# Second batch's sums, sketches and numerators at other places among the down projections, and a weight chunk's splitting one unit sooner

## The chip, the cores and the metric

The kernel runs on one core of a Trainium2 chip. The metric is the device time of one execution in microseconds (us): the median of three runs of the kernel before is 279.8 us (279.78 to 281.41). Each engine of the core takes its own instructions from its own queue: PE (TensorE) multiplies matrices, DVE (VectorE) and ACT (ScalarE) do elementwise work and copies, POOL (GpSimd) does elementwise work between buffers in SBUF, and SP (SyncE) issues DMAs. PE writes its results to PSUM, which here is eight banks of 128 x 512 floats; the kernel calls two neighbouring banks a pair.

## The reference

```python
def phi(x):                        # sketched features, r*r = 64 per token
    a = np.einsum('rd,bhsd->bhsr', S1, x)
    b = np.einsum('rd,bhsd->bhsr', S2, x)
    return np.einsum('bhsi,bhsj->bhsij', a, b).reshape(*x.shape[:-1], r * r)
q_p, k_p = phi(q), phi(k)
kv  = np.einsum('bhsf,bhsd->bhfd', k_p, v)
z   = np.sum(k_p, axis=2)
num = np.einsum('bhsf,bhfd->bhsd', q_p, kv)
den = np.einsum('bhsf,bhf->bhs', q_p, z)[..., None] + 1e-06
x   = (num / den).transpose(0, 2, 1, 3).reshape(4352, 128)
g   = x @ w_gate                   # 128 x 1536
out = (g / (1 + np.exp(-g)) * (x @ w_val)) @ w_out
```

There are four batches of 4 heads x 1088 tokens x 32 channels. The output is 4352 x 128 in float32.

## The kernel before

The first batch's attention is done by itself at the start. From then on the feed-forward part (FFN) sets the pace, and the attention of the later batches is cut into steps that are placed between its pieces.

The tokens form blocks. Blocks 0, 1 and 2 are the first batch (384, 320 and 384 tokens); blocks 3 (`HEAD`) onward have 480 tokens each, the last one fewer. The 1536 hidden channels form 12 columns `j` of 128, and the weights are kept in four chunks of three columns. One unit is one block with one column: gate and value products, silu of the gate, and their product, which is a hidden slice. One `down` (line 1054) multiplies one hidden slice by its part of `w_out` and adds into the block's PSUM bank; the block's twelfth `down` is followed by `store` (line 1127), a DVE transpose and four DMAs on SP.

Units come in two forms. Those of blocks 0 and 1, and the first three of block 2, are plain float32 (`unit`, line 1017). From unit 3 of block 2 on, each product is the sum of faster fp32r products of split operands. `start_unit` (line 983) issues the two products with the difference parts and an ACT pass that negates the two banks (line 992). `finish_unit` (line 994) issues the four other products (lines 1001 and 1002), then ACT takes the silu (line 1004), and DVE makes the hidden slice (line 1009) and thereby frees the unit's pair. The split parts come from `cut_weights` (line 839), four steps for a chunk (ACT line 843, DVE or POOL line 846, ACT line 848, DVE or POOL line 855/851), and from `cut_tokens` (line 857) for a block: x1 on ACT (line 865), xd on DVE (line 873) and x0 on DVE or POOL (line 868). With `soon=True` the order is x1, xd, and in the next step x0.

No scheduler reorders anything: instructions stand in each engine's queue in the order in which the Python code issues them. A semaphore wait is added wherever an operand comes from another engine. A bank or buffer is reused only once its last reader is done; `pair` (line 122) hands out the pair that was least recently used among those not held.

The attention of batches 1 to 3 is the generator `attentions` (line 615), advanced one step by each `parts_of(1)` (line 1252). These steps of the second batch (batch 1) matter here:

- the step with the key sums: `key_values` (line 388), the third batch's `key_products` (line 354) and its ACT copies (line 590), `value_sums` (line 713, PE, which needs `zs`, the POOL sums of line 547), `fold` (DVE, lines 601 to 608, which makes the operand `s123` of the query sketches) and `spread_out` (a DVE transpose on line 723, six DMAs on SP, and four loads of the next values);
- the step with the query sketches: `query_sketches` (line 342, PE) and two ACT copies into `qab`;
- eight steps of `query_step` (line 737): scores and division (lines 741 to 748), then three times a product (line 377) and a transpose (line 758) on DVE, which fill `phT`;
- `numerators` (line 766): 64 small matmuls (line 776) into two pairs, then copies to `xT` (line 793) on ACT and DVE. These are the tokens of block 3 and beyond.

Three loops place all this. The first (`for z`, line 1327) runs the plain units. The second (`for n in range(ND)`, line 1354) has 19 `down`s; after the `down` numbered n it takes an attention step if n is in a listed set, and the splitting steps that `steps_at[n]` names ("x" is `cut_tokens` of block 2, "g3" and "v3" are chunk 3 of the gate and value weights). The third (`for j in range(3, NCH)`, line 1366) runs the nine split units of block 2. Its turn j starts unit j + 1, finishes unit j, takes a `down`, and then steps. A last `while` loop takes the rest of the `down`s and starts block 3.

Of the kernel before, what the change touches and what calls it, by code (L numbers as in the profile page):

```python
# [19 lines left out]
def kernel(  # L20
# [38 lines left out]
    NCH = Dff // P  # L59
# [62 lines left out]
    def pair(keep=None):  # L122

        i = min((i for i in (0, 4, 6) if i not in held), key=lambda i: max(used[i], used[i + 1]))
        touch(i, i + 1)
        if keep is not None:
            held.add(i)
            kept[keep] = i
        return PS[:, i : i + 2, :]
# [3 lines left out]
    def let_go(keep):  # L133
        i = kept.pop(keep)
        held.discard(i)
        touch(i, i + 1)
# [720 lines left out]
    def cut_tokens(i, engine=nc.gpsimd, soon=False):  # L857

        t0, n = blocks[i]
        x = xT[:, t0 : t0 + n]  # L860
        x1, x0, xd = x_parts[i] = [
            apool.tile([P, WB], F32R, tag=tag, name=name, bufs=2)
            for tag, name in (("qb", "x1"), ("dT", "x0"), ("rd", "xd"))
        ]
        nc.scalar.activation(x1[:, 0:n], x, AF.Copy, scale=CUT)  # L865

        def low():
            engine.tensor_tensor(  # L868
                out=x0[:, 0:n], in0=x, in1=whole(x1[:, 0:n]), op=ALU.subtract
            )  # L870

        def difference():
            nc.vector.scalar_tensor_tensor(
                out=xd[:, 0:n], in0=whole(x1[:, 0:n]), scalar=WHOLE, in1=x,
                op0=ALU.mult, op1=ALU.subtract,
            )


        first, second = (difference, low) if soon else (low, difference)
        first()  # L880
        yield
        second()
# [16 lines left out]
    def now(where, y):  # L899
        for f in where.pop(y, ()):  # L900
            f()
# [49 lines left out]
    def cut_hidden(y, i, j):  # L951

        if not h_sets:
            x = []
            for tag in ("kld", "qld", "vld", "kT", "qT"):
                t = const.tile([P, 2, WB], F32R, tag=tag, name="h" + tag, bufs=1)
                x += [t[:, k, :] for k in range(2)]
            t = const.tile([P, 8, WB], F32R, tag="late", name="hlate", bufs=1)
            x += [t[:, k, :] for k in range(8)]
            h_sets.extend(x[k : k + 3] for k in range(0, 18, 3))  # L960
        n = SPLIT if i == LAST else blocks[i][1]
        h_sets.append(h_sets.pop(0))
        h1, h0, hd = h_parts[i, j] = [x[:, 0:n] for x in h_sets[-1]]
        h = hidden[i, j][:, 0:n]
        if j in (2, 5, 8, 10) and i != line[2]:
            add_to(before, y + 1, lambda: nc.vector.tensor_scalar(h1, h, CUT, None, op0=ALU.mult))
        else:
            add_to(behind, y + 1, lambda: nc.scalar.activation(h1, h, AF.Copy, scale=CUT))  # L968
        add_to(before, y + 2, lambda: nc.gpsimd.tensor_tensor(  # L969
            out=h0, in0=h, in1=whole(h1), op=ALU.subtract  # L970
        ))
        add_to(before, y + 3, lambda: nc.vector.scalar_tensor_tensor(
            out=hd, in0=whole(h1), scalar=WHOLE, in1=h, op0=ALU.mult, op1=ALU.subtract
        ))
# [8 lines left out]
    def start_unit(i, j):  # L983

        n = blocks[i][1]
        xd = x_parts[i][2][:, 0:n]
        ps = sums_of[i, j] = pair((i, j))[:, :, 0:n]
        for k, w in enumerate((wg, wv)):
            nc.tensor.matmul(  # L989
                ps[:, k], w_parts[id(w), j // 3][2][:, j % 3, :], xd, start=True, stop=True  # L990
            )
        nc.scalar.activation(ps, ps, AF.Copy, scale=-1.0 / WHOLE)  # L992

    def finish_unit(i, j, y=None):
        n = blocks[i][1]
        x1, x0, _ = (x[:, 0:n] for x in x_parts[i])
        ps = sums_of.pop((i, j))
        now(before, y)
        for k, w in enumerate((wg, wv)):
            w1, wb = (w_parts[id(w), j // 3][t][:, j % 3, :] for t in range(2))  # L1000
            nc.tensor.matmul(ps[:, k], w1, x1, start=False, stop=False, skip_group_check=True)  # L1001
            nc.tensor.matmul(ps[:, k], wb, x0, start=False, stop=True, skip_group_check=True)  # L1002
        sg = fpool.tile([P, WB], FP32, tag="sg", name="sg", bufs=5)[:, 0:n]
        nc.scalar.activation(sg, ps[:, 0], AF.Silu, scale=WHOLE)  # L1004
        slot_of[i, j] = slots.pop(0)
        hj = slot_of[i, j]
        hidden[i, j] = hj
        todo.append((i, j))
        nc.vector.scalar_tensor_tensor(  # L1009
            out=hj[:, 0:n], in0=ps[:, 1], scalar=WHOLE, in1=sg, op0=ALU.mult, op1=ALU.mult  # L1010
        )
        let_go((i, j))
        now(behind, y)
        if (i, j) in DOWN:
            cut_hidden(y, i, j)
# [38 lines left out]
    def down(y=None):  # L1054

        i, j = todo.pop(0)
        n = SPLIT if i == LAST else blocks[i][1]
        first = i not in acc
        if first:
            acc[i] = bank("g2" if i == 1 or i in line[2::2] else "acc")  # L1060
        made[i] = made.get(i, 0) + 1
        mine = [c for c in range(NCH) if (i, c) in DOWN]
        if mine and j == mine[0]:
            acc[i, "p"] = bank("acc" if i in line[2::2] else "g2")
        sides = dict(start=first, stop=(made[i] == NCH))
        if j in mine:
            w1, wb, wd = [down_parts[x][:, FINE.index(j), :] for x in ("w1", "wb", "wd")]
            h1, h0, hd = h_parts.pop((i, j))
            nc.tensor.matmul(acc[i][:, 0:n], wd, hd, **sides)  # L1069
            p = acc[i, "p"][:, 0:n]  # L1070
            nc.tensor.matmul(p, w1, h1, start=(j == mine[0]), stop=False)  # L1071
            nc.tensor.matmul(p, wb, h0, start=False, stop=(j == mine[-1]))  # L1072
            if j == mine[-1]:
                copy_out(y, i, n)
        else:
            w = down_parts["scaled"][:, PLAIN.index(j), :] if mine else wo[:, j, :]
            nc.tensor.matmul(acc[i][:, 0:n], w, hidden[i, j][:, 0:n], **sides)  # L1077
        if i != LAST:
            hidden.pop((i, j))
            slots.append(slot_of[i, j])  # L1080
        if made[i] == NCH:
            if mine:
                put_together(y, i, n)
            elif i == HEAD - 1:

                add_to(behind, 1, lambda: store(i, n))
            else:
                store(i, n)
# [62 lines left out]
    def part(name, i):  # L1151

        next(fills[name, i], None)
# [47 lines left out]
    n = steps[0][1]  # L1201
# [50 lines left out]
    def parts_of(n):  # L1252

        for _ in range(n):
            if ahead[0] not in ("pe", "end"):
                ahead[0] = next(att, "end")
# [60 lines left out]
    def at(*names):  # L1317
        for name in names:
            next(cuts[name], None)

    def next_down():
        if order:
            todo.remove(order[0])
            todo.insert(0, order.pop(0))
        down()

    for z, (i, j) in enumerate(seq):
# [19 lines left out]

    steps_at = {
        0: ("v1", "v2"), 1: ("g1",), 2: ("g2",), 3: ("g1", "v1", "v2"), 4: ("g1",), 5: ("g1", "g2"), 6: ("g2", "v1"),
        7: ("g2", "v2"), 8: ("v3",), 9: ("g3",), 10: ("v0",), 11: ("g0",), 12: ("x",), 13: ("x",), 14: ("g3",),  # L1350
        15: ("g3",), 18: ("g3",),
    }
    ND = 19
    for n in range(ND):
        if n == ND - 2:
            start_unit(2, 3)
        next_down()
        for p in parts.pop(len(seq) + n, ()):
            part(*p)
        parts_of(n in (0, 1, 2, 3, 4, 11, 13, 15, 16, 17))  # L1360
        at(*steps_at.get(n, ()))


    steps_at = {4: ("v3",), 6: ("v3",), 7: ("v3",), 8: ("v0", "g0"), 9: ("v0", "g0"), 10: ("v0", "g0")}
    todo.sort(key=lambda x: (order + [x]).index(x))
    for j in range(3, NCH):
        if j + 1 < NCH:
            start_unit(2, j + 1)
        else:
            parts_of(1)  # L1370
            x_steps = cut_tokens(HEAD, nc.vector, soon=True)
            next(x_steps)
        finish_unit(2, j)
        next_down()
        parts_of(j < 8)
        if j == 4:


            lows["v3"][:] = [slots.pop().rearrange("p (c f) -> p c f", f=P)]
        at(*steps_at.get(j, ()))  # L1380
    while todo:
        if len(todo) == 2:
            start_unit(HEAD, 0)
        next_down()
        next(x_steps, None)
        parts_of(len(todo) > 0)

    flat = hbuf[:].rearrange("p s w -> p (s w)")
# [73 lines left out]
```

## Time and profile before

| quantity | value |
|---|---|
| median of the three runs | 279.8 us |
| the profiled execution's own time | 279.75 us |
| its span in the profile | 278.0 us |
| PE busy | 269.6 us (97% of the span) |
| DVE / ACT / POOL busy | 213.7 / 193.9 / 99.2 us |
| granted TensorE clock | full in all 40 slices |

The span runs from the first to the last recorded instruction, so 1.75 us of the execution lie around it. Times in a timeline count from the span's start. A row merges neighbouring instructions of one kind: start, length, engine, source line, operation, result and operands, shape, and count; brackets give the idle time of the engine just before the row and what ended it. For a float32 matmul PE shows two records per instruction, so "x4" on line 1077 is two `down`s. The records of successive matmuls overlap[...]: a row's start and the start of the next one tell more than its length.

### The profile page before, as it was taken

To read this page: it belongs to the slowest core of one execution; us is meant where nothing else is said; L and a number is where in the kernel's file an instruction comes from. 1 tells how busy PE (TensorE), PEld (TensorE's weight loads), DVE (VectorE), ACT (ScalarE), POOL (GpSimd) and SP (SyncE) were. 2 spreads that over 40 slices of the span, in tenths; PEclk is the share of its full clock that TensorE was granted. 3 is DMA by queue.
4 is the path that set the end of the run, shared out by engine and by line. 5 is a ranking of instruction groups with operands and counts; after the bars stand their busy time and mean duration, and the time that the engine had idled before them with its cause. 6 is when DMAs were issued, how large, how long until landed. Compare 5 with 4: busy or idle time off the path is not lost.

```text
span 278.0 us, 5775 instructions
## 1 busy us (share of the span) xinstructions
PE 269.6 (97%) x2193; PEld 201.4 (72%) x2193; DVE 213.7 (77%) x371; ACT 193.9 (70%) x348; POOL 99.2 (36%) x111
## 2 busy tenths in 40 slices
PE   8899999996999999999999999999999999999995
PEld 7645566664886677767667778767887888788994
DVE  3997988999896883787736667867986995978771
ACT  3468566444676676766568898859879888887880
POOL 3314322179020360080024352435335462633320
PEclk9999999999999999999999999999999999999999
DMA  6573195222250033200200010000100200010021
GB/s 194 165 229 95 37 283 170 83 80 83 60 90 0 4 61 90 58 0 0 35 13 6 4 30 6 0 2 8 28 2 0 35 1 0 12 26 1 5 33 28
DMA packets 26139, 14.30 MB, mean 51 GB/s; under 512 B 19840, under 2 KB 24192, under 8 KB 26112
## 3 DMA queue, kind: packets, MB, share of 16 engines
q1 hardware_dynamic: 25456, 13.84, 19.5%
q8 instruction: 17, 0.28, 0.4%
q10 hardware_dynamic: 656, 0.10, 0.2%
q14 instruction: 10, 0.08, 0.1%
HBM read 11.41 MB, written 2.23 MB: 49 GB/s over the span
## 4 chain that ended last, share of the span: by engine, by line
PE 86%; DVE 7%; POOL 2%; DMA 2%; issue 1%; ACT 1%; SPq 0%; DVEq 0%; ACTq 0%; POOLq 0%
PE PS L1077 17%; PE PS L1001 14%; PE PS L989 14%; PE PS L1002 13%; PE PS L1025 10%; PE PS L1069 3%; PE PS L1072 3%; PE PS L1071 3%; PE PS L776 2%; PE PS L342 2%; POOL zs L547 2%; DMA kld<-in_k_dram 2%; PE PS L354 1%; DVE phk L377 1%; PE PS L388 1%
## 5 line engine op out<-in xcount | busy, mean ns | idle before, releaser
L992 ACT ACTIVATE PS<-PS 128x960 f32<-128x960 f32 (+1 forms) x93 | 85.7, 922 | 33.0 <-PE PS L989 32.0
L1009 DVE SCALAR_TENSOR_TENSOR hbuf<-PS,sg 128x480 f32<-128x480 f32 (+1 forms) x93 | 58.5, 629 | 40.5 <-ACT sg L1004 38.3
L1004 ACT ACTIVATE sg<-PS 128x480 f32<-128x480 f32 (+1 forms) x93 | 51.1, 549 | 1.3 <-PE PS L1002 1.2
L1077 PE MATMUL PS<-hbuf,wo 128*128 128x480 f32 (+2 forms) x100 | 41.6, 518 | 0.0
L989 PE MATMUL PS<-xd,graw 128*128 128x480 f32 (+1 forms) x72 | 39.9, 554 | 0.0
L989 PE MATMUL PS<-xd,wd 128*128 128x480 f32 (+1 forms) x93 | 34.5, 371 | 0.2 <-DVE hbuf L1009 0.2
L1002 PE MATMUL PS<-x,wb 128*128 128x480 f32 (+1 forms) x93 | 34.5, 371 | 0.0
L1001 PE MATMUL PS<-x,w 128*128 128x480 f32 (+1 forms) x93 | 34.4, 370 | 0.0
L1002 PE MATMUL PS<-x,graw 128*128 128x480 f32 (+1 forms) x72 | 26.6, 369 | 0.0
L989 PEld LDWEIGHTS PS<-xd,wd 128*128 128x128 f32 x93 | 17.6, 189 | 11.3 <-issue 5.9
L1077 PEld LDWEIGHTS PS<-hbuf,wo 128*128 128x128 f32 x100 | 18.7, 189 | 5.1 <-issue 0.4
L1025 PE MATMUL PS<-xT,wg 128*128 128x384 f32 (+1 forms) x54 | 21.1, 472 | 0.1
L1025 PE MATMUL PS<-xT,wv 128*128 128x384 f32 (+1 forms) x54 | 20.7, 466 | 0.3 <-DVE wv L286 0.3
L1077 PE MATMUL PS<-hbuf,scaled 128*128 128x480 f32 (+1 forms) x48 | 20.7, 518 | 0.0
L868 POOL TENSOR_TENSOR x<-xT,x 128x480 fp32r<-128x480 f32 (+1 forms) x6 | 7.1, 1192 | 37.7 <-ACT x L865 37.7
L989 PEld LDWEIGHTS PS<-xd,graw 128*128 128x128 f32 x72 | 13.6, 189 | 8.1 <-ACT PS L992 4.1
L1001 PEld LDWEIGHTS PS<-x,w 128*128 128x128 f32 x93 | 17.5, 188 | 2.2
L1002 PEld LDWEIGHTS PS<-x,wb 128*128 128x128 f32 x93 | 17.5, 188 | 2.1
L969 POOL TENSOR_TENSOR hlate<-hbuf,hlate 128x480 fp32r<-128x480 f32 (+1 forms) x12 | 14.3, 1198 | 11.4 <-ACT hlate L968 9.3
L1001 PE MATMUL PS<-x,graw 128*128 128x480 f32 (+1 forms) x48 | 18.1, 376 | 0.0
L1029 ACT ACTIVATE sg<-PS 128x384 f32<-128x384 f32 (+1 forms) x21 | 9.6, 462 | 11.1 <-PE PS L1025 11.1
L1001 PE MATMUL PS<-x,gphq 128*128 128x480 f32 (+1 forms) x45 | 17.0, 377 | 0.0
(201 smaller groups left out, 546.7 us busy)
## 6 DMA issues: line engine op xcount, KB each, us to landing
kld<-in_k_dram SPq DMA_DIRECT2D x4, 544.0 KB, 4.2
vld<-in_v_dram SPq DMA_DIRECT2D x12, 144.0 KB, 5.2
qld<-in_q_dram SPq DMA_DIRECT2D x3, 544.0 KB, 4.0
raw<-in_moe_w_out_dram SPq DMA_DIRECT2D x4, 384.0 KB, 4.4
raw<-in_moe_w_gate_dram SPq DMA_DIRECT2D x3, 384.0 KB, 3.7
raw<-in_moe_w_val_dram SPq DMA_DIRECT2D x3, 384.0 KB, 3.5
out_dram<-o SPq DMA_DIRECT2D x16, 60.0 KB, 2.0
vld<-in_v_dram SPq DMA_DIRECT2D x4, 112.0 KB, 4.2
```

The lines of the kernel that those rows point to most:

```text
L969: add_to(before, y + 2, lambda: nc.gpsimd.tensor_tensor(out=h0, in0=h, in1=whole(h1), op=ALU.subtract))
L989: nc.tensor.matmul(ps[:, k], w_parts[id(w), j // 3][2][:, j % 3, :], xd, start=True, stop=True)
L992: nc.scalar.activation(ps, ps, AF.Copy, scale=-1.0 / WHOLE)
L1001: nc.tensor.matmul(ps[:, k], w1, x1, start=False, stop=False, skip_group_check=True)
L1002: nc.tensor.matmul(ps[:, k], wb, x0, start=False, stop=True, skip_group_check=True)
L1004: nc.scalar.activation(sg, ps[:, 0], AF.Silu, scale=WHOLE)
L1009: nc.vector.scalar_tensor_tensor(out=hj[:, 0:n], in0=ps[:, 1], scalar=WHOLE, in1=sg, op0=ALU.mult, op1=ALU.mult)
L1025: nc.tensor.matmul(o[:, 0:n], w[:, j, :], xT[:, t0 : t0 + n], start=True, stop=True)
L1029: nc.scalar.activation(sg[:, 0:n], g[:, 0:n], AF.Silu)
L1069: nc.tensor.matmul(acc[i][:, 0:n], wd, hd, **sides)
L1071: nc.tensor.matmul(p, w1, h1, start=(j == mine[0]), stop=False)
L1077: nc.tensor.matmul(acc[i][:, 0:n], w, hidden[i, j][:, 0:n], **sides)
```

## The change

The step with the key sums is taken after `down` 13 in place of 11 of the second loop. The query sketches follow after `down` 16 in place of 13, so three `down`s lie between the two steps in place of two. The remaining attention steps of that loop follow after 17 and 18. The first step of "x" (x1 and xd) is issued with n = 11 and the second (x0) with n = 12, in place of 12 and 13. In the third loop the attention steps go on through j = 8. The numerators come at j = 10, in front of the end of unit 10 and the start of unit 11, with two `down`s behind it, where before they came at j = 11, in front of the end of unit 11. The splitting steps of "v3" are taken at j = 3, 5 and 6 in place of 4, 6 and 7, and one "g0" step moves from j = 10 to j = 9. x0 of block 3 is issued at the end of turn j = 11, where before the `while` loop issued it. Nothing is added or removed: every product, copy and DMA is the same as before.

```diff
-        7: ("g2", "v2"), 8: ("v3",), 9: ("g3",), 10: ("v0",), 11: ("g0",), 12: ("x",), 13: ("x",), 14: ("g3",),
+        7: ("g2", "v2"), 8: ("v3",), 9: ("g3",), 10: ("v0",), 11: ("g0", "x"), 12: ("x",), 14: ("g3",),
         15: ("g3",), 18: ("g3",),
     }
...
-        parts_of(n in (0, 1, 2, 3, 4, 11, 13, 15, 16, 17))
+        parts_of(n in (0, 1, 2, 3, 4, 13, 16, 17, 18))
         at(*steps_at.get(n, ()))
...
-    steps_at = {4: ("v3",), 6: ("v3",), 7: ("v3",), 8: ("v0", "g0"), 9: ("v0", "g0"), 10: ("v0", "g0")}
+    steps_at = {3: ("v3",), 5: ("v3",), 6: ("v3",), 8: ("v0", "g0"), 9: ("v0", "g0", "g0"), 10: ("v0",)}
     todo.sort(key=lambda x: (order + [x]).index(x))
+    x_steps = iter(())
     for j in range(3, NCH):
-        if j + 1 < NCH:
-            start_unit(2, j + 1)
-        else:
+
+        alone = j == NCH - 2
+        if alone:
             parts_of(1)
             x_steps = cut_tokens(HEAD, nc.vector, soon=True)
             next(x_steps)
-        finish_unit(2, j)
-        next_down()
-        parts_of(j < 8)
-        if j == 4:
+            finish_unit(2, j)
+        if j + 1 < NCH:
+            start_unit(2, j + 1)
+        if not alone:
+            finish_unit(2, j)
+        for _ in range(1 + alone):
+            next_down()
+        parts_of(j < 9 or j == NCH - 1)
+        if j == 3:
             lows["v3"][:] = [slots.pop().rearrange("p (c f) -> p c f", f=P)]
         at(*steps_at.get(j, ()))
+        if j == NCH - 1:
+            next(x_steps, None)
     while todo:
         if len(todo) == 2:
             start_unit(HEAD, 0)
         next_down()
-        next(x_steps, None)
         parts_of(len(todo) > 0)
```

As built, the queues of the changed kernel differ from those of the kernel before at these places. On PE two `down`s of 384 tokens stand in front of the key products in place of behind the value sums, and three of 320 tokens stand between the value sums and the query sketches in place of behind the sketches. On DVE xd, x0 and the store transpose of block 0 stand in front of the fold. On ACT a gate weight's split and x1 stand in front of the two copies of the key sketches. On SP the four output DMAs of block 0 stand in front of the six `spread` DMAs and the four value loads.

## The prediction

> **What bounds the kernel now.** I read the page first, then PE's timeline around the moved steps, then DVE's and ACT's over the same stretch. The page says that the end is set by PE:
>
> ```profile
> PE 269.6 (97%) x2193; PEld 201.4 (72%) x2193; DVE 213.7 (77%) x371; ACT 193.9 (70%) x348; POOL 99.2 (36%) x111
> PE 86%; DVE 7%; POOL 2%; DMA 2%; issue 1%; ACT 1%; SPq 0%; DVEq 0%; ACTq 0%; POOLq 0%
> ```
>
> So a moved step gains or loses only what it does to PE's gaps. In the moved stretch PE shows these:
>
> ```profile
> 62.80 1.21 PE L388 MATMUL PS<-phk,vld 128*32 128x64 f32 x72
> 63.94 0.80 PE L354 MATMUL PS<-s,kT 128*64 128x64 f32 x20
> 65.15 0.69 PE L354 MATMUL PS<-s,kT 128*64 128x64 f32 x16 [0.41 <-DVE kT L327]
> 67.66 0.32 PE L713 MATMUL PS<-zs,ones 128*32 128x64 f32 x8 [1.82 <-POOL zs L547]
> 67.91 1.56 PE L1077 MATMUL PS<-late,wo 128*128 128x384 f32 x4
> 69.39 1.69 PE L342 MATMUL PS<-s,qT 128*32 128x96 f32 x72
> 71.02 1.88 PE L1077 MATMUL PS<-late,wo 128*128 128x320 f32 x6
> 72.49 0.58 PE L989 MATMUL PS<-xd,graw 128*128 128x384 f32 x1
> ...
> 87.65 2.35 PE L776 MATMUL PS<-phT,spread 32*32 32x288 f32 x64
> ...
> 97.61 0.48 PE L989 MATMUL PS<-xd,wd 128*128 128x480 f32 x1 [0.23 <-DVE hbuf L1009]
> ```
>
> The reader is to see two gaps before the first split unit, 0.41 + 1.82 = 2.23 us, and that PE goes from the value sums to the sketches without one: the two downs at 67.91 hide the fold. From 72.49 to 87.65 there is no gap. The numerators take 2.28 us (87.65 to 89.93) where the fourth batch's take 1.49 (185.34 to 186.83 in the chain): 0.79 of it is a stall, since their second pair is freed by the DVE product that runs from 87.88 to 88.44 below. DVE and ACT over the same time:
>
> ```profile
> 67.05 0.97 DVE L851 SCALAR_TENSOR_TENSOR graw<-room,graw 128x384 fp32r<-128x384 f32 x1
> 68.04 0.23 DVE L601 TENSOR_TENSOR fold<-PS,sq 128x64 f32<-128x64 f32 x1
> ...
> 68.88 0.24 DVE L723 STREAM_TRANSPOSE spread<-PS 128x64 f32<-128x64 f32 x1
> 70.27 0.56 DVE L873 SCALAR_TENSOR_TENSOR xd<-x,xT 128x384 fp32r<-128x384 f32 x1 [1.15 <-ACT x L865]
> 70.74 0.58 DVE L1131 STREAM_TRANSPOSE o<-PS 128x384 f32<-128x384 f32 x1
> 71.24 0.52 DVE L868 TENSOR_TENSOR x<-xT,x 128x384 fp32r<-128x384 f32 x1
> ...
> 87.88 0.56 DVE L1009 SCALAR_TENSOR_TENSOR hbuf<-PS,sg 128x384 f32<-128x384 f32 x1 [1.37 <-ACT sg L1004]
> ```
>
> ```profile
> 68.72 0.68 ACT L590 COPY kab<-PS 128x320 f32<-128x320 f32 x2
> 69.29 0.53 ACT L843 ACTIVATE gphq<-wg 128x384 fp32r<-128x384 f32 x1
> 69.72 0.52 ACT L865 ACTIVATE x<-xT 128x384 fp32r<-128x384 f32 x1
> ```
>
> The fold starts 0.02 us after DVE's previous work. xd waits for ACT's x1, which is late because ACT itself was waiting for DVE before 67.05.
>
> **What the Trainium skill says.** "Perfetto Trace Analysis", section on the Tensor Engine instruction: DVE, ACT and GpSimd take their queues strictly in order, and a matmul's end is a computed one. The first decides this case, and the trace agrees as far as it can: no DVE row overtakes xd in its 1.15 us wait. The second is why I count from start to start. "SBUF — State Buffer", "Who interferes with whom": DVE and GpSimd share a port pair under an exclusive lock. The trace agrees: the weight remainder (line 846) took 1.62 us beside GpSimd's sums at 62.85, and 0.55 at 71.68 without them.
>
> **The change, part by part.** Every instruction exists before; only waits change.
>
> *Two downs in front of the key sums.* A down of 384 tokens costs 0.65 us in the chain, so the key products start at 62.80 + 1.30 = 64.10. They take 1.14 and the key sketches 1.2, the end being 66.44; kT is ready at 65.10, so the 0.41 gap goes. The POOL queue is unchanged and zs still lands at 67.61, so PE waits 1.2 in place of 1.82 and the value sums start at 67.66 as before. The gain is the 1.30 us of downs that no longer follow.
>
> *Three downs behind the value sums.* 320 tokens cost 0.54 each, 1.62 together: PE reaches the sketches at 67.91 + 1.62 = 69.53.
>
> *x1, xd and x0 sooner.* The sketches need the fold, and the fold now stands on DVE behind xd, x0 and the store of block 0. ACT, released at 67.05, has one more weight split in front of x1: starts 0.42 apart (67.05, 67.48, 67.89, 68.31, 68.72) put x1 at 69.14 and its end at 69.66. DVE idles from 68.02 until then. xd at 69.69, x0 at 70.16, store at 70.62 and fold at 71.12 follow with the old starts' spacing (0.47, 0.44 to 0.50). The fold's chain lasted 0.92 (68.04 to 68.96), which ends at 72.04. PE therefore waits from 69.53 to about 72.05, 2.5 us. Behind it stand all split units; behind the fold on DVE the spread transpose and the scores. The sketches (1.63) end at 73.68 and the first split product follows, not at 72.49: 1.2 late. In terms: 1.30 of downs gained in front, 2.5 of wait paid. Bounds of the wait: x1 follows four splits on an ACT that is released at 67.05, at 0.41 or more each, so x1 can hardly end before 69.4 and the wait is at least 2.2; if the three DVE steps slow as beside GpSimd (0.97 against 0.55), it is at most 3.5.
>
> *SP.* The four stores are issued at about 0.5 us each (eight took 3.95 at 76.11), so the spread DMAs end near 78 plus 3.7 to land at worst. The numerators need them at 87; the value loads are needed at 100. Cost nothing; without that cover, up to 2 us.
>
> *Query step.* The ACT copies end 2.24 after the sketches' start (71.63 - 69.39), hence 74.3; the scores follow 2.1 later than before. The weight step and unit 3's product now stand ahead of the feature products, so unit 3's product is at 77.1, when its silu is ready (75.91 + 1.2). Products and transposes (0.87 each) alternate with the 1.69 us units and catch up: the last transpose runs 85.9 to 86.8 behind unit 8's product.
>
> *Chunk 3's GpSimd steps.* wd (line 855) ended at 82.35, just before its product at 82.37, with no gap. Sooner gains nothing, and at worst GpSimd's 1.0 us lands beside another DVE product (1.80 in place of 0.96 at 81.37), which the slack before 85.4 takes.
>
> *Numerators in front of unit 10.* PE gets there at 87.73 - 1.69 + 1.2 = 87.2. Their second pair is unit 9's, whose DVE product stands behind the transpose and two weight remainders (0.46 and 0.5): it starts near 87.75 and ends near 88.3. The stall is 1.1 in place of 0.79, +0.3. Afterwards all three pairs are taken, so unit 11's first product waits for ACT's copies (0.81 after the end of the numerators, PE arriving at 0.80: +0.06), and unit 11's finish waits for ACT's pass behind copies, x1 and a silu (ends 2.65 after; PE arrives at about 2.5: +0.2). Block 3's start has 4.7 us of cover in place of 2.45, but no gap was there. The gap of 0.23 at 97.61, where DVE was late with the key features, mostly vanishes as PE is later: -0.2.
>
> *Sum.* 1.2 + 0.3 + 0.26 - 0.2 = 1.56 us. From 98 us on PE is full and nothing takes it back. The profiled execution becomes 279.75 + 1.56 = 281.3; its 279.75 is within 0.05 of the 279.8 median, so the same number stands for both.
>
> **The rivals.** (1) The gain comes as drawn: the fold is not held. Then the first split product is 1.33 early (67.91 + 1.62 + 1.63 = 71.16), and with 0.3 + 0.26 later the time is 279.75 - 1.33 + 0.56 = 279.0; 278.4 if those are absent too. For it: PE's two gaps are real. Against: x1's end at 69.66. (2) Slower, over 1%: the late scores make phT late. If GpSimd's lock stretches two feature products by 0.9 each behind the wait, the last transpose ends near 88.3, unit 9's product near 89.8, and the numerators stall 2.5 (+1.7); with the 0.26 behind them and no recovery at 97.61 that is 1.2 + 1.7 + 0.26 = 3.1, or 282.9. It decides once unit 9's product ends 1.1 us later than the 88.3 above. For it: 1.80 us seen at 81.37. Against: each unit leaves DVE 0.4 us spare. (3) The second half gives it back: DVE has caught up, unit 9's product ends before PE arrives at 87.2, and the old stall goes: 1.2 - 0.79 - 0.2 = +0.2, 280.0. Against: the two weight remainders stand in front of that product, which puts its end at 88.3.
>
> **How the numbers follow.** Main case 0.62, rival 1 0.09, rival 2 0.2, rival 3 0.09. The main case with its wait of 2.2 to 3.5 gives 281.0 to 282.3. The range 279.4 to 282.8 adds rival 3 and the near part of rival 2, and leaves out rival 1 and some 0.1 of rival 2. A change under 1% can hardly be told from none: faster (below 277.0) 0.02, within 0.78, slower (above 282.6) 0.20.
>
> **What would show it.** In the profile after: a gap in front of line 342 of about 2.5 us whose releaser is DVE, xd on DVE ahead of the fold with a wait on ACT line 865 of about 1.6 us, the gap before line 713 down to 1.2, and the numerators at 2.5 us or more. I am wrong if line 342 starts before 71, or if the numerators take over 3.3 us.

## The result, and the profile after

The changed kernel takes 281.6 us (median of 20 runs, 280.94 to 282.96), the kernel before beside it 281.49 us (20 runs, 279.60 to 282.54). The ratio is 1.0021 with a 95% interval of 1.0001 to 1.0041: some 0.6 us slower, and within 1%. The profiled execution of the changed kernel took 280.94 us with a span of 279.2 us, where the one of before took 279.75 with 278.0: 1.2 us more.

One fact is needed to read these numbers: in part of the executions the granted TensorE clock dips for a short time, which shows as a mean clock of 0.988 to 0.994 in place of 0.998 or more, and these are about 1.5 us longer. Of the changed kernel, 11 of 20 executions ran at the full clock (median 281.22) and 9 had a dip (282.73). For these 20 of the kernel before only times are on record: 4 lie at 279.6 to 280.2 (median 279.79) and 16 at 281.3 to 282.5, which I take for executions with a dip. The times alone don't part them sharply: of 46 later executions of that kernel at the full clock, 10 took over 281 us as well. Like against like the change costs 1.2 us (the two profiles, both at the full clock) to 1.4 (the medians). It reads as 0.6 in the whole because fewer of its executions have a dip. Where the dips come from is tried below.

The page of the changed kernel still names PE, with the same work:

```profile
PE 269.7 (97%) x2193; PEld 200.8 (72%) x2193; DVE 213.2 (76%) x371; ACT 194.2 (70%) x348; POOL 99.4 (36%) x111
```

PE's timeline of the changed kernel, over the moved steps (start, length, line, operation, result and operands, idle time before and its releaser):

```profile
63.94 1.21 PE L388 MATMUL PS<-phk,vld 128*32 128x64 f32 x72
65.08 1.27 PE L354 MATMUL PS<-s,kT 128*64 128x64 f32 x36
67.49 0.32 PE L713 MATMUL PS<-zs,ones 128*32 128x64 f32 x8 [1.14 <-POOL zs L547]
67.73 1.88 PE L1077 MATMUL PS<-late,wo 128*128 128x320 f32 x6
71.77 1.69 PE L342 MATMUL PS<-s,qT 128*32 128x96 f32 x72 [2.15 <-DVE s L608]
73.39 0.44 PE L989 MATMUL PS<-xd,graw 128*128 128x384 f32 x1
...
86.72 0.68 PE L776 MATMUL PS<-phT,spread 32*32 32x288 f32 x6
87.89 1.51 PE L776 MATMUL PS<-phT,spread 32*32 32x256 f32 x58 [0.50 <-DVE hbuf L1009]
```

The two gaps of before, 0.41 and 1.82 us, have become one of 1.14. A new one of 2.15 stands in front of the query sketches, released by the last DVE instruction of the fold. DVE and ACT show why the fold is so late:

```profile
66.89 0.96 DVE L851 SCALAR_TENSOR_TENSOR graw<-room,graw 128x384 fp32r<-128x384 f32 x1
69.51 0.57 DVE L873 SCALAR_TENSOR_TENSOR xd<-x,xT 128x384 fp32r<-128x384 f32 x1 [1.66 <-ACT x L865]
70.00 0.55 DVE L868 TENSOR_TENSOR x<-xT,x 128x384 fp32r<-128x384 f32 x1
70.47 0.57 DVE L1131 STREAM_TRANSPOSE o<-PS 128x384 f32<-128x384 f32 x1
70.97 0.18 DVE L601 TENSOR_TENSOR fold<-PS,sq 128x64 f32<-128x64 f32 x1
71.19 0.27 DVE L605 TENSOR_REDUCE w<-fold 128x8 f32<-128x64 f32 x1
71.49 0.22 DVE L608 TENSOR_TENSOR s<-w,own 128x64 f32<-128x64 f32 x1
...
86.39 0.52 DVE L846 TENSOR_TENSOR room<-wv,w 128x384 f32<-128x384 f32 x1
86.83 0.55 DVE L846 TENSOR_TENSOR room<-wg,gphq 128x384 f32<-128x384 f32 x1
87.29 0.55 DVE L1009 SCALAR_TENSOR_TENSOR hbuf<-PS,sg 128x384 f32<-128x384 f32 x1
```

```profile
68.55 0.51 ACT L843 ACTIVATE gphq<-wg 128x384 fp32r<-128x384 f32 x1
68.97 0.51 ACT L865 ACTIVATE x<-xT 128x384 fp32r<-128x384 f32 x1
```

The value sums start at 67.49, so the fold could have started near 67.9 (before it started 0.38 us behind them). It stands behind xd, which waits 1.66 us for x1, behind x0 and behind the store. At 86.39 two weight remainders stand in front of unit 9's product, which ends at 87.84, and only then does the larger part of the numerators run.

The first stage differs by up to 1.6 us from one profiled execution to the next, so I count each from the first row of its last plain unit (line 1025, 128x320). The end of the count is the third batch's key products. Two rows of before, then two of the changed kernel:

```profile
53.78 0.81 PE L1025 MATMUL PS<-xT,wg 128*128 128x320 f32 x2
100.21 1.21 PE L388 MATMUL PS<-phk,vld 128*32 128x64 f32 x72
...
53.63 0.81 PE L1025 MATMUL PS<-xT,wg 128*128 128x320 f32 x2
101.38 1.21 PE L388 MATMUL PS<-phk,vld 128*32 128x64 f32 x72
```

The starts of PE's rows then are:

| us after the last plain unit | before | after | difference |
|---|---|---|---|
| key products with the values, line 388 | 9.02 | 10.31 | +1.29 |
| value sums, line 713 | 13.88 | 13.86 | 0.0 |
| query sketches, line 342 | 15.61 | 18.14 | +2.53 |
| first split product, line 989 | 18.71 | 19.76 | +1.05 |
| length of the numerators' stretch | 2.28 | 2.61 | +0.33 |
| end of the numerators to block 3's first product | 2.45 | 4.49 | +2.04, of it 1.69 a unit that now lies there |
| third batch's key products, line 388 | 46.43 | 47.75 | +1.32 |

### The profile page after: what moved, and what is told of

The parts are those of the page before. It is cut to its first block, busy times and chain, and to the rows that moved or that the text cites. A ratio compares the mean times of both kernels' runs of the same rounds, so it can differ in the third digit from the quotient of the medians.

```text
span 279.2 us, 5778 instructions
## 1 busy us (share of the span) xinstructions
PE 269.7 (97%) x2193; PEld 200.8 (72%) x2193; DVE 213.2 (76%) x371; ACT 194.2 (70%) x348; POOL 99.4 (36%) x111
## 4 chain that ended last, share of the span: by engine, by line
PE 86%; DVE 9%; ACT 1%; DMA 1%; issue 1%; SPq 0%; ACTq 0%; DVEq 0%
PE PS L1077 17%; PE PS L1001 14%; PE PS L989 14%; PE PS L1002 14%; PE PS L1025 10%; PE PS L1072 3%; PE PS L1071 3%; PE PS L1069 3%; PE PS L776 2%; PE PS L342 2%; DMA kld<-in_k_dram 1%; PE PS L354 1%; DVE room L846 1%; PE PS L388 1%; DVE man L277 1%; PE PS L1117 1%
```

## Experiments: the hold in front of the sketches

**The token split behind the fold.** This moves x1, xd and x0 so far that the sums' step is issued ahead of them.

```diff
-        ... 11: ("g0", "x"), 12: ("x",), 14: ("g3",),
+        ... 11: ("g0",), 13: ("x",), 14: ("x", "g3"),
```

> Block 2's token split one down later than the changed kernel has it, so that x1, xd and x0 stand behind the fold in their queues; all else as changed. My theory (the fold is held on DVE behind xd, which waits for x1): the 2.15 us gap in front of the query sketches goes, since only the store transpose (0.57) stands in front of the fold and the three downs (1.62) hide both. The first split unit starts 2.2 us sooner than in the changed kernel and 1.2 sooner than before; the numerators still stall, so the span is 279.2 - 2.1 = 277.1 and the time about 278.8. Rival (the gap comes from elsewhere, from the downs moved in front or from zs): the gap stays at 1 us or more and the span within 0.7 us of 279.2.

Measured: 279.87 us (20 runs), ratio to before 0.9952 (0.9935 to 0.9968), span 278.5. PE and DVE of this kernel:

```profile
68.15 0.32 PE L713 MATMUL PS<-zs,ones 128*32 128x64 f32 x8 [1.15 <-POOL zs L547]
68.40 1.88 PE L1077 MATMUL PS<-late,wo 128*128 128x320 f32 x6
70.47 1.69 PE L342 MATMUL PS<-s,qT 128*32 128x96 f32 x72 [0.18 <-DVE s L608]
...
74.40 0.44 PE L1001 MATMUL PS<-x,gphq 128*128 128x384 f32 x1 [0.27 <-ACT PS L992]
```

```profile
68.94 0.18 DVE L601 TENSOR_TENSOR fold<-PS,sq 128x64 f32<-128x64 f32 x1
69.16 0.27 DVE L605 TENSOR_REDUCE w<-fold 128x8 f32<-128x64 f32 x1
69.46 0.95 DVE L608 TENSOR_TENSOR s<-w,own 128x64 f32<-128x64 f32 x1
```

The gap of 2.15 is down to 0.18, and the first split product comes 17.81 us after the last plain unit in place of 19.76: 1.95 sooner, with 2.2 expected. The 0.18 is left because line 608 took 0.95 us here and 0.22 in the changed kernel: GpSimd is splitting weights (line 855) at that time. The third batch's key products come at 46.35, 1.40 sooner and not 2.1. The missing 0.5 is the wait at 74.40: unit 3's end follows its predecessor by 0.60 where it was 0.17, and its next product follows by 0.28 where it was 0.18. PE got there before ACT had done the sketches' copies and the negation:

```profile
72.30 0.52 ACT L848 ACTIVATE graw<-room 128x384 fp32r<-128x384 f32 x1 [1.56 <-DVE room L846]
72.73 0.92 ACT L590 COPY qab<-PS 128x480 f32<-128x480 f32 x2
```

The copies start 2.26 us after the sketches, where it was 1.10 in the changed kernel (71.77 to 72.87). They stand behind a weight split that waited for a remainder on DVE, and that remainder (line 846, at 71.71) stands behind xd and x0. So by the trace the 0.5 goes back to DVE's order too; no run tried that wait by itself. The hold in front of the sketches is shown to be the order on DVE, and of the 1.95 us that it cost, 0.5 is lost again at ACT when it goes. This version costs nothing against the kernel before at the full clock (46.35 against 46.43).

**One instruction taken out of the hold at a time.** First x0 alone behind the fold, then the weight split alone behind x1:

```diff
-        ... 11: ("g0", "x"), 12: ("x",), 14: ("g3",),
+        ... 11: ("g0", "x"), 13: ("x",), 14: ("g3",),                 # x0 behind the fold
+        ... 11: ("x",), 12: ("x",), 13: ("g0",), 14: ("g3",),         # the split behind x1
```

> The changed kernel with only x0 (one DVE instruction, start to start 0.47 us) moved from in front of the fold to behind it; x1 and xd stay in front. If the hold is the sum of what stands in DVE's queue behind the wait for x1, the gap in front of the sketches falls from 2.15 to 1.68 us. If it is set by something else that ends near then, it stays at 2.15.

> The changed kernel with the first split of chunk 0's gate weights (one ACT instruction, start to start 0.41 us) moved from in front of x1 to two downs later. If the hold begins with x1's place in ACT's queue, DVE's wait falls from 1.66 to 1.25 us and the gap in front of the sketches from 2.15 to 1.74 us. If ACT's queue is not the start of it, both stay.

Measured with x0 behind, on PE:

```profile
71.88 1.69 PE L342 MATMUL PS<-s,qT 128*32 128x96 f32 x72 [1.68 <-DVE s L608]
```

That is the 1.68 expected, and the third batch's key products come 0.44 sooner (47.31). With the split behind x1, DVE and PE show:

```profile
69.35 0.99 DVE L873 SCALAR_TENSOR_TENSOR xd<-x,xT 128x384 fp32r<-128x384 f32 x1 [1.24 <-ACT x L865]
70.27 0.54 DVE L868 TENSOR_TENSOR x<-xT,x 128x384 fp32r<-128x384 f32 x1
```

```profile
72.03 2.33 PE L342 MATMUL PS<-s,qT 128*32 128x96 f32 x72 [2.15 <-DVE s L608]
```

DVE's wait fell by the 0.41 expected, to 1.24. The gap did not fall at all: xd, started sooner, ran beside GpSimd's weight split and took 0.99 in place of 0.57. ACT's queue is where the hold begins, but of a lead of 0.42 us there nothing was left. Its time of 282.85 us has a clock dip in it, which comes below; the dip begins at about 72.9, behind the gap. Both are single runs.

## Experiments: the two halves

**The second loop as changed, the third as before; and the other way round.** The first takes the changed sums, sketches and token split with the numerators at their old place, the second the reverse.

```diff
 # first half alone: the kernel before, with
-        parts_of(n in (0, 1, 2, 3, 4, 11, 13, 15, 16, 17))
+        parts_of(n in (0, 1, 2, 3, 4, 13, 16, 17, 18))
...
-        parts_of(j < 8)
+        parts_of(j < 9)
 # and the first steps_at of the changed kernel; second half alone: the changed kernel, with
-        parts_of(n in (0, 1, 2, 3, 4, 13, 16, 17, 18))
+        parts_of(n in (0, 1, 2, 3, 4, 11, 13, 15, 16, 17))
...
-        parts_of(j < 9 or j == NCH - 1)
+        parts_of(j < 8 or j == NCH - 1)
 # and the first steps_at of the kernel before
```

> The second loop as changed (sums, sketches and x moved), the third loop as before (numerators in front of unit 11's end, chunk 3's steps at the old turns). My theory: this half holds the 1.05 us by which the first split unit was late, and about nothing more; the numerators stall 0.8 as before: span 278.0 + 1.0 = 279.0. Rival (the third loop's half costs most of it): span below 278.5.

> The second loop as before, the third loop as changed. My theory: no gap in front of the sketches, the numerators stall about 0.9 to 1.1 in place of 0.8, unit 11's end waits 0.2, the 0.23 us gap behind may go: span 278.0 + 0.2 to 0.5, about 278.3. Rival (the third loop's half costs most of it): span above 278.7.

Measured for the first half, in a single run at the full clock: span 279.8, third batch's key products at 47.77, so +1.34, all of the change's 1.32. Its numerators take 2.71 us, so they did not stall "0.8 as before" but 1.2, and my figure of 1.0 for this half was too small. Measured for the second half, also a single run: span 279.4 at a mean clock of 0.993. PE's rows, and the busy times by stretch (the stretch, its length, the busy time and count of PE, PE's weight loads, DVE, ACT and POOL, the granted clock, the DMA share, GB/s):

```profile
67.69 0.44 PE L713 MATMUL PS<-zs,ones 128*32 128x64 f32 x8 [1.82 <-POOL zs L547]
68.06 2.93 PE L1077 MATMUL PS<-late,wo 128*128 128x384 f32 x4
70.92 1.69 PE L342 MATMUL PS<-s,qT 128*32 128x96 f32 x72
```

```profile
64.00:66.00 2.00, 1.47 (x40) 1.20 (x36) 2.00 (x4) 0.52 (x1) 1.84 (x3) 1.00 0.03 8
66.00:67.60 1.60, 0.00 (x0) 0.00 (x0) 1.56 (x3) 0.52 (x2) 1.52 (x3) 0.97 0.79 239
67.60:69.00 1.40, 1.31 (x10) 0.84 (x11) 1.19 (x5) 1.40 (x5) 1.40 (x3) 0.50 0.31 124
69.00:70.00 1.00, 1.00 (x3) 0.54 (x2) 0.15 (x1) 1.00 (x4) 0.87 (x1) 0.50 0.00 0
70.00:71.00 1.00, 1.00 (x6) 0.08 (x8) 0.56 (x1) 0.26 (x1) 0.00 (x0) 0.55 0.12 25
71.00:72.00 1.00, 1.00 (x52) 1.00 (x56) 0.97 (x3) 0.00 (x0) 0.00 (x0) 1.00 0.12 25
```

The reader is to see the clock at 0.50 behind the gap of 1.82 us. The means (0.97, 0.50, 0.50, 0.55) make 3.4 us at half, from about 67.5, in the last 0.2 us of the gap, to about 70.9. The two downs at 68.06 take 2.86 us to the next row, where in the profile of before they take 1.48; with the value sums (0.37 against 0.25) that is 1.5 us. Taking it off, the second half alone ends 0.2 us ahead of the kernel before (47.74 - 1.50 = 46.24 against 46.43), and its numerators take 2.04. So by span the rival came true (above 278.7), but not for its reason: what the span holds is a stretch of PE at half clock. My own theory failed too, since the stall is 0.55 (2.04 against 1.49) in place of 0.9 to 1.1: with DVE not late, the two remainders in front of unit 9's product hold up nothing.

**The weight remainders behind unit 9's product.**

```diff
-    steps_at = {3: ("v3",), 5: ("v3",), 6: ("v3",), 8: ("v0", "g0"), 9: ("v0", "g0", "g0"), 10: ("v0",)}
+    steps_at = {3: ("v3",), 5: ("v3",), 6: ("v3",), 9: ("v0", "g0", "v0", "g0"), 10: ("v0", "g0")}
```

> The changed kernel with the two weight remainders of chunk 0 (DVE line 846) one turn later, behind unit 9's product in place of in front of it. My theory (they hold up unit 9's product, for which the numerators' second pair waits): unit 9's product starts 0.6 us sooner, the numerators' stall falls from 1.1 to about 0.5, span 279.2 - 0.6 = 278.6, less if the later gap of 0.2 us behind block 3's first product comes back (278.8). Rival (the stall is set by unit 9's silu on ACT, or the loss is given back later): the span stays within 0.2 of 279.2.

The later steps of the same two splits move along with the remainders. Measured in a single run at the full clock, DVE and PE:

```profile
87.19 0.56 DVE L1009 SCALAR_TENSOR_TENSOR hbuf<-PS,sg 128x384 f32<-128x384 f32 x1 [0.25 <-ACT sg L1004]
87.67 0.55 DVE L846 TENSOR_TENSOR room<-wv,w 128x384 f32<-128x384 f32 x1
```

```profile
87.20 2.11 PE L776 MATMUL PS<-phT,spread 32*32 32x288 f32 x64
89.24 0.44 PE L1001 MATMUL PS<-x,graw 128*128 128x384 f32 x1
```

Unit 9's product now waits for its own silu, and the numerators' stretch falls from 2.61 to 2.04. The third batch's key products come at 47.21, 0.54 sooner, and the span is 279.1 with a start 0.45 us later. By the span alone this would read as the rival; counted from the last plain unit, the theory holds. The remainders were the hold.

## Experiments: the clock

**Filling PE's gap in the kernel before.** The filling matmuls multiply constants into the unused second bank of the pair that holds the key sums.

```diff
         run_copies(copies, 2)
+        keep_warm(8, ps=kvz[:, 1, :])
         value_sums(kvz[:, 0, :], zs)
```

> The kernel before with eight bfloat16 matmuls of 512 columns (about 0.22 us each, results unused) on PE in the 1.82 us gap in front of the value sums; nothing else changed. New theory, formed from the granted clocks (20 of the executions timed so far of the kernel before lie near 281.5 us with a mean granted clock of 0.994, few near 279.7 with 1.0): PE's idle stretch at 65.8 to 67.7 lets the granted clock fall to half for some 3 us, which costs about 1.6 us in most executions. Then filling the gap keeps the clock and the median becomes 279.8 to 280.2, nearly all executions at 1.0, a ratio of about 0.994. Rival (the slower group has another cause, such as the chip or the start): the ratio stays within 0.998 to 1.002 and most executions stay near 0.994.

Measured: all 20 executions at 0.998 or more, median 280.13 (279.46 to 282.12); ratio to before 0.9975 (0.9955 to 0.9995). The kernel before beside it had 38 of 69 executions at 0.988 to 0.994 (median 281.51), the other 31 have a median of 280.30. PE's rows:

```profile
67.19 1.91 PE L241 MATMUL PS<-const-bfloat16-1.0 128*32 128x512 bf16 x8
69.08 0.32 PE L714 MATMUL PS<-zs,ones 128*32 128x64 f32 x8
```

The value sums come 13.85 us after the last plain unit (13.88 before) and the third batch's key products at 46.40 (46.43), so nothing but PE's idleness was changed, and the dips are gone. The median lies in the range expected (279.8 to 280.2). The ratio is nearer to 1 than the 0.994 expected, since in these runs fewer executions of the kernel before had a dip (38 of 69, against 18 of 23 beside the token-split kernel).

**Filling the gap in front of the sketches in the changed kernel.** Nine such matmuls in front of `query_sketches`; the gap of 1.15 in front of the value sums stays.

```diff
+        keep_warm(9, ps=spare[0])          # spare[0]: the same unused bank
         qab, copies = sketched(pair(), query_sketches, 3, "qab")
```

> The changed kernel with nine bfloat16 matmuls of 512 columns (results unused, about 2 us) on PE in the 2.15 us gap in front of the query sketches; the 1.14 us gap in front of the value sums stays. In 9 of 20 executions of the changed kernel the mean granted clock was 0.992 to 0.994 and the time 1.5 us longer. If the clock dip comes from the long gap in front of the sketches: nearly all executions at 0.998 or more and 281.0 to 281.6, median about 281.3, against before a ratio near 1.000. Rival (the dip comes from the shorter gap in front of the value sums, or from both together): some four to nine of 20 executions stay at 0.994 and 282.7.

Measured: 281.5 us, ratio 1.0018 (0.9999 to 1.0036); 19 of 20 executions at 0.998 or more (median 281.48), one at 0.992. The third batch's key products stand at 47.75 as in the changed kernel, which had 11 of 20 at the full clock. That was another set of runs, beside which the kernel before dipped somewhat more often (some 16 of 20, here 13 of 23); the fall from 9 of 20 to 1 of 20 is more than that. So the dips of the changed kernel come from the new gap, not from the one of 1.15. One is seen in a trace, in the kernel with the weight split behind x1, behind that gap (69.88 to 72.03):

```profile
70.00:72.00 2.00, 0.00 (x0) 0.00 (x0) 1.93 (x7) 0.32 (x1) 0.00 (x0) 1.00 0.00 0
72.00:74.00 2.00, 1.97 (x72) 1.97 (x72) 0.57 (x2) 1.08 (x2) 0.00 (x0) 0.73 0.56 88
74.00:76.00 2.00, 2.00 (x15) 1.49 (x6) 1.01 (x3) 1.15 (x2) 0.00 (x0) 0.50 0.18 35
76.00:78.00 2.00, 2.00 (x10) 1.68 (x9) 1.39 (x4) 0.80 (x2) 0.00 (x0) 0.92 0.08 16
```

The clock is still full in the gap. The means (0.73, 0.50, 0.92) again make 3.4 us at half, but from about 72.9 on, 0.9 us after the gap's end. The price is 1.61 us: the third batch's key products stand at 49.36, against 47.75 in the changed kernel with the same gap. The kernel whose gaps there are 1.15, 0.18 and 0.27 us (the token split behind the fold) had no dip in 20 executions.

## Experiments: versions that are faster

**Both holds taken away,** that is the token split behind the fold and the remainders behind unit 9's product; **the token split behind with the old third loop;** and **a third down in front of the sums,** on top of the first of these:

```diff
-        parts_of(n in (0, 1, 2, 3, 4, 13, 16, 17, 18))
+        parts_of(n in (0, 1, 2, 3, 4, 14, 17, 18))
+        if n == ND - 2:
+            start_unit(2, 3)               # no longer in front of the down
...
-        parts_of(j < 9 or j == NCH - 1)
+        parts_of((j < 9) + (j == 3) + (j == NCH - 1))
```

with "x" after n = 14 and 15, and the second "g3" step after 16.

> The changed kernel with both holds taken away: block 2's token split one down later (behind the fold) and chunk 0's weight remainders one turn later (behind unit 9's product). The two are at different places, so they should add: key products of the third batch 1.4 + 0.5 = 1.9 us sooner than in the changed kernel, counted from the last plain unit, and 0.6 sooner than before. Against executions of the kernel before at full clock (279.7) about 279.2; and since PE's longest gap is then 1.15 us, no clock dips: median 279.3, a ratio of 0.992 to 0.994. Rival (later stages give it back): as the kernel with the first alone, 279.9.

> The first half of the change with the token split behind the fold, and the third loop as before: numerators at their old place. If the place of the numerators costs nothing by itself (the second half alone came out 0.14 us sooner than before once its clock dip is taken off), the key products of the third batch stand within 0.2 us of the kernel that has only the token split moved back (46.35 us after the last plain unit), median about 279.9. If the new place is what pays once the first part is 1 us earlier, this one is 0.5 us or more later.

> The kernel with both holds taken away, and a third down moved in front of the key sums, with the sketches one down later, and unit 3's start behind them. My theory (the gap in front of the value sums, 1.15 us, is slack of the sums on GpSimd, and each down moved in front fills 0.54 of it): gap down to 0.6, key products of the third batch another 0.5 us sooner, median about 278.8, ratio 0.990. Rival (unit 3's start then waits for ACT's copies of the sketches, and the gap only moves): no better than the kernel with both holds taken away.

| kernel | median us | ratio to before | third batch's key products at |
|---|---|---|---|
| token split behind the fold | 279.87 | 0.9952 (0.9935 to 0.9968) | 46.35 |
| the same, third loop as before | 279.79 | 0.9958 (0.9940 to 0.9975) | 46.37 |
| both holds taken away | 279.32 | 0.9945 (0.9925 to 0.9964) | 45.75 |
| and a third down in front | 279.65 | 0.9942 (0.9925 to 0.9959) | 46.11 |

None of these had an execution below 0.998. The two holds add: 1.40 + 0.54 = 1.94 us, and 2.00 are measured. The place of the numerators costs nothing by itself (46.37 against 46.35). The third down shortens the gap in front of the value sums as expected (1.15 to 0.62), but unit 3's end then comes too soon for ACT, and it is the rival that holds:

```profile
67.85 0.32 PE L713 MATMUL PS<-zs,ones 128*32 128x64 f32 x8 [0.62 <-POOL zs L547]
...
74.09 0.44 PE L1001 MATMUL PS<-x,gphq 128*128 128x384 f32 x1 [0.80 <-ACT PS L992]
```

Here too the sketches' copies start 2.26 us after the sketches (70.16 to 72.42), behind the weight split that waits for DVE. The version with both holds taken away is the fastest by its median and by PE's timeline; by the ratio it and the one with the third down can't be told apart. Against the kernel before it gains 0.68 us at the full clock by PE's timeline (46.43 - 45.75); the rest of its 0.55% I put down to the dips that it doesn't have.

## Why the prediction was right, and where it was not

- *The hold on the fold:* right, step by step. Counted from the last plain unit, x1, xd, x0, the store and the fold start within 0.03 us of the times predicted, and DVE's wait for x1 is 1.66 ("about 1.6"). The gap of 2.15 us in the trace is counted from the modelled end of the last down; from start to start, as the prediction counts, it is 71.77 - (67.73 + 1.62) = 2.42, where 2.5 was predicted. The fold's own chain was oversized: 0.92 us in the profile of before and 0.74 here (70.97 to 71.71), since before line 608 overlapped GpSimd's weight split, and here GpSimd had finished.
- *The downs in front of the sums:* right. The gap of 1.82 fell to 1.14 (1.2 predicted), the other went, and the first split product is 1.05 late (1.2 predicted). Of this 1.05, 0.14 is only a matter of rows: before, the first split product's row began beside the downs in front of it, and the second split unit followed it by 1.43 us in place of 1.29.
- *SP and chunk 3's steps at no cost:* nothing contradicts this; neither shows up as a releaser of PE. One reading was off without harm: the product that needs wd starts at 82.67 in the profile of before, its weight load at 82.50, not at 82.37.
- *The numerators:* their size was right, the reason only in part. The stretch of 2.61 us has a stall of 1.1, +0.33 (predicted +0.3), unit 11 adds 0.35 (predicted 0.26), and 0.27 comes back behind block 3's first products (predicted 0.2). But I put this on the move of the numerators. The first half alone, with the old place, loses as much (47.77 against 47.75), and the second half alone, with the new place, stalls less than before (2.04 against 2.28). What costs is that DVE comes late out of the second loop and then has the two remainders in front of unit 9's product: with the remainders behind it, or with DVE not late, the stretch is 2.04. At the old place the path is longer: there unit 10's product waits 1.23 us for its silu on ACT, where a weight split had waited for the same remainders. That path is read from the trace and was not tried.
- *The sum:* 1.05 - 0.14 + 0.33 + 0.35 - 0.27 = 1.32 us by PE's timeline where 1.56 was predicted, and 280.94 for the profiled execution where 281.3 was; the median of the 11 executions at the full clock is 281.22.
- *The step that failed:* "its 279.75 is within 0.05 of the 279.8 median, so the same number stands for both". In twenty runs the kernel before has a median of 281.49, since most of its executions have a clock dip behind the old gap of 1.82 us; one of the three times shown was 281.41. The changed kernel dips in fewer. The prediction has no term for the clock. So the ratio moved by 0.6 us in place of 1.56, and that the new median of 281.6 lies near 281.3 is partly luck: had the changed kernel dipped as often as the one before, some 16 of 20, its median would by estimate have been near the 282.73 of those that did.
- *The rivals:* the first (no hold) and the third (the second half gives it back) are excluded by the gap and by the stall. The second, GpSimd's lock on the feature products, did occur (one took 1.80 us at 80.44), but unit 9's product ended at 87.84, and DVE's slack took it as predicted.

## What to carry to other kernels

When work is moved to close one engine's gap, follow what is moved with it in every other in-order queue: here x1, xd and x0 went one down sooner, and the fold that PE waits for got behind them. Price a gap by its length and by what the clock does behind it; two executions at different granted clocks don't compare, and a few profiles don't tell how often each occurs. Where two engines contend, a lead on one can vanish on the next.

## What the runs showed of the hardware

- In two traced executions the granted clock was 0.50 for 3.4 us at a PE gap, at a price of 1.5 to 1.6 us: from the last 0.2 us of a gap of 1.82 us on (0.7 us behind one of 0.41), and from 0.9 us after a gap of 2.15 us on. By the mean clock, 69 of 115 executions of the kernel before and 9 of 20 of the changed one had a dip; filling the gap left none of 20 and 1 of 20. The four kernels of the table, whose gaps in the moved stretch are at most 1.15 us, had none in 78 executions (the profile of one of them has a gap of 1.32 us in the first stage, at 6.64). The Trainium skill ("TensorE: Matmul & The Clock Gate", "HAM oscillation") warns of gaps above about 3.4 us; the measurement here decides, and gaps that are shorter matter. What picks the executions is open; it was not tried.
- One DVE instruction on 64 elements a partition (line 608) took 0.22 us by itself and 0.95 beside a GpSimd operation.
